# Score matmuls of a windowed attention, cut into 32 queries by the 96 keys that they see

## The chip, the cores and the metric

The kernel runs on one core of one Trainium2 chip. The metric is the device time of one execution in microseconds (us), as the median of several runs. The core has five engines that matter here: TensorE (PE in the profile, its weight loads PEld), VectorE (DVE), ScalarE (ACT), GpSimd (POOL) and SyncE (SP, which issues the DMA transfers).

## What is computed

```python
# q, k, v: (8 batches, 8 heads, 576 positions, 64), float32
scores = matmul(q, k^T) / sqrt(64)
rel = pos[:, None] - pos[None, :]
scores = where((rel >= 0) & (rel < 64), scores, -1e9)
attn = exp(scores - max(scores))
attn = attn / (sum(attn) + 1e-9)
x = matmul(attn, v), heads side by side           # (4608, 512)
h = maximum(x @ w_in, 0.0)                        # w_in (512, 2048)
out = (h * h) @ w_out                             # w_out (2048, 512)
```

A query sees itself and the 63 keys before it. So a block of 64 queries sees keys of its own block and of the block before, 128 in all; the first 32 queries of the block see only the first 96 of these, the last 32 only the last 96.

## The kernel before

The 4608 tokens are taken in 12 tiles of 384. Attention runs in sections: a section is four items, an item being one block of 64 queries of one batch for four heads (`d` picks the group of four, `j` and `hd` the head in it). A tile has three sections, so there are 36. Everything is one function, `section(op, i)`, with one letter per step:

- S, the scores (L227 to 238): for each item, for `j` and for `hd`, one 32-bit matmul of 64 queries by 128 keys (64 keys where the block is the first of its sequence). The head's 64 channels lie in partitions 0 to 63 or 64 to 127, and the output goes to partitions 0 to 63 or 64 to 127 of one of two PSUM banks: `half = hd ^ j`. So four neighbouring matmuls use the four 64x64 quarters of the 128x128 array.
- o and s (L246, L255, L256): ScalarE copies the scores of the own block out of PSUM, VectorE puts the scores of the block before over those that lie in the future. Each score that is kept comes from one of the two halves by the mask `late`.
- z, y, e, f, k, R, m: maximum (L258), exponential (L266), sum, reciprocal (L272), and on GpSimd the weighing by it (L275).
- X and x: TensorE transposes the weights (L279), VectorE masks them into `pt` (L283).
- V, the values (L301): 64 channels by 64 or 128 queries, again in 64x64 quarters.
- H and Q: the result leaves PSUM as operand of the feed-forward part (L316, L318).

The feed-forward part consists of wide products over the full array in a rounded 32-bit form with a high and a low part. Four tiles go the plain way: `mm1` (L407) and `mm2` (L449). The other eight go in pairs by seven products instead of eight: `product` (L940), `second` (L1038), and for the last pair `fast` (L1189).

What sets the order: up to about 190 us a list of tokens written out by hand (S, V, M for `mm1`, O for `mm2`, ...). After that a planner: `plan(engine, cost, do, reads, writes)` collects the steps; TensorE's steps keep the order in which they were planned, and each step of another engine gets a due time, which is the sum of TensorE's costs up to the step that needs it less its own cost. The earliest due goes first among those that are ready. `burst(i, j)` (L832) plans the scores of section i and right behind them the values of an earlier section j; `cross(i)` (L817) plans the transposes some products later.

```python
def scores(i):
    ...
    plan("pe", 0.85, by(section, "S", i), [("qk", d, j) for d in range(2) for j in range(2)], ["s_ps"])
...
def burst(i, j):
    scores(i)
    values(j)
    weigh(i)
    settle(j)
```

Of the kernel before, what the change touches and what calls it, by code (L numbers as in the profile page):

```python
# [14 lines left out]

P = 128
QB = 64
TB = 6
TT = QB * TB
SW = 4  # L20
# [9 lines left out]
def window_attention_relu2_ffn(ctx: ExitStack, tc: tile.TileContext, q, k, v, w_in, w_out, out):  # L30
    nc = tc.nc
    pe, dve, act, pool, sp = nc.tensor, nc.vector, nc.scalar, nc.gpsimd, nc.sync
    B, H, S, D = q.shape
    NT, DM = out.shape
    DF = w_in.shape[1] // 2
    NPAIR = H // 2
    NB = S // QB
    NF = DF // P
# [14 lines left out]
    banks = psum.tile([P, 8, DM], F32, name="banks")  # L53
    raw_t = att.tile([P, 2, 2, S], F32, name="raw")
    vt_t = att.tile([P, (NB + 1) // 2, 2, H // 2, D], F32, name="vt")
    qk_t = att.tile([P, 2, 2, 2, S], F32, name="qk")
    sel_t = att.tile([P, 2, SW, 2, QB], F32, name="sel")
    pt_t = att.tile([P, 2 * SW, P], F32, name="pt")
# [21 lines left out]

    late = const.tile([P, 1, QB], F32, name="late")
    masks = const.tile([P, 2, 2, QB], F32, name="masks")
    neg = const.tile([P, 1], F32, name="neg")
    nc.vector.memset(neg, NEG)
    for m, first_value, other, sign in ((late, 0.0, 1.0, 1), (masks[:, 1], 1.0, 0.0, -1), (masks[:, 0], 0.0, 1.0, -1)):
        nc.gpsimd.memset(m, first_value)
        for hd in range(2):
            rows = m[hd * QB:(hd + 1) * QB]
            nc.gpsimd.affine_select(out=rows, in_=rows, pattern=[[0, m.shape[1]], [-sign, QB]], base=0,
                                    channel_multiplier=sign, compare_op=ALU.is_ge, fill=other)  # L90
# [133 lines left out]
    def section(op, i, eng=None):  # L224
# [3 lines left out]
        if op == "S":  # L228
            ps = ps_s[i] = banks[:, 0:2]
            for w, (b, qb, d) in enumerate(items):  # L230
                c0 = 0 if qb else QB
                k0 = max(qb - 1, 0) * QB
                for j in range(2):
                    qk = (first[b][:, d] if b in first and qb < FIRST // QB else turned[b, d])[:, j]
                    for hd in range(2):
                        r = slice(hd * D, (hd + 1) * D)
                        half = hd ^ j
                        pe.matmul(ps[half * QB:(half + 1) * QB, j, w * P + c0:(w + 1) * P],  # L238
                                  lhsT=qk[r, 0, qb * QB:(qb + 1) * QB], rhs=qk[r, 1, k0:k0 + P - c0], start=True, stop=True)
            nms[i] = nm_t[:, 0, i % 3]  # L240
            sums[i] = nm_t[:, 1, i % 3]
        elif op in "os":
# [18 lines left out]
        elif op in "ef":  # L261
            for w in range(SW // 2):
                w += "ef".index(op) * SW // 2
                for hd in range(2):
                    n = slice(2 * w + hd, 2 * w + hd + 1)
# [7 lines left out]
        elif op == "m":  # L273
            p = sels[i].rearrange("p w h c -> p (w h) c")
# [11 lines left out]
        elif op == "V":  # L286

            ps = ps_x[i] = banks[:, 2:4]
# [6 lines left out]
            for m, (b, kb, d, n0, n) in enumerate(todo):  # L295
                q0 = n0 // 2 * QB
                for j in range(2):
                    for hd in range(2):
                        r = slice(j * QB, (j + 1) * QB)
                        half = hd ^ j  # L300
                        pe.matmul(ps[hd * D:(hd + 1) * D, j, q0:q0 + n * QB],  # L301
                                  lhsT=vts[b, kb // 2][r, kb % 2, 2 * d + hd, :],
                                  rhs=pts[i][r, n0:n0 + n, half * QB:(half + 1) * QB],
                                  start=m == 0, stop=m == len(todo) - 1, skip_group_check=True)
            pts.pop(i)
        else:
            hi, lo = get_x(i // SPT)
            ps = ps_x[i].rearrange("p m (w q) -> p m w q", q=QB)
            for d, nd, w0, r0, n in regions:
                cols = slice(r0 * QB, (r0 + n) * QB)  # L310
                h, l = hi[:, :, d:d + nd, cols], (hi if lo is None else lo)[:, :, d:d + nd, cols]
                vals = ps[:, :, w0:w0 + nd * n].rearrange("p m (d r) q -> p m d (r q)", d=nd)
                if nd == 1:
                    h, l, vals = h[:, :, 0], l[:, :, 0], vals[:, :, 0]
# [8 lines left out]
    def plan_tile(t):  # L323
        blocks = [divmod(t * TB + r, NB) for r in range(TB)]
        if t < 2:
            cuts = [[(d, r + n) for d in range(2) for n in range(2)] for r in range(0, TB, 2)]
        elif blocks[0][0] == blocks[-1][0]:
            order = [(d, r) for d in range(2) for r in range(TB)]
            cuts = [order[n:n + SW] for n in range(0, 2 * TB, SW)]
        else:  # L330
            cuts = [[(0, 0), (0, 1), (0, 2), (1, 0)], [(1, 1), (1, 2), (0, 3), (0, 4)], [(0, 5), (1, 3), (1, 4), (1, 5)]]
        for cut in cuts:
            at = [n for n, (d, r) in enumerate(cut) if blocks[r][1] == 0]
            if at and t > 1:
                cut = cut[at[0]:] + cut[:at[0]]
            regions = []
            for n, (d, r) in enumerate(cut):
                if n and cut[n - 1] == (d, r - 1):
                    regions[-1][4] += 1
                else:  # L340
                    regions.append([d, 1, n, r, 1])
            if len(regions) == 2 and regions[0][3:] == regions[1][3:]:
                regions = [[0, 2, 0, *regions[0][3:]]]
            yield [(*blocks[r], d) for d, r in cut], regions

    secs = [x for t in range(NTILE) for x in plan_tile(t)]
    SPT = 2 * TB // SW
    xt = {}
# [201 lines left out]
    with tc.manual_schedule(engines={E.PE, E.DVE, E.Activation, E.Pool, E.SP}):  # L550
        for token in order.split():
            op, eng = token[0], token[-1] if token[-1] in "dap" else None
            n = int(token[1:].rstrip("dap"))
# [8 lines left out]
            elif op == "D":  # L562
                turn(1 + n // NPAIR, n % NPAIR)
            elif op in "TU":
                ps_f[op, n] = turn_first("TU".index(op), *divmod(n, 2))
            elif op in "tu":
                copy_first("tu".index(op), *divmod(n, 2), ps_f[op.upper(), n], copier(eng))
            elif op == "K":
                idle(n)
            elif op == "P":  # L570
                fetch_w(0, n)
            elif op in "JjY":
                weight("abc"["JjY".index(op)], 0, half=n)
            elif op in "abcdhl":
                weight(op, n, eng)
            elif op == "M":
                hs[n] = mm1(*steps[n], lambda kk, part, f=steps[n][1]: wparts[f][:, 0, part, kk * P:(kk + 1) * P])
            elif op in "rpgG":
                evac(op, n, eng)
            elif op == "B":  # L580
                keep(n)
            elif op in "ACEF":
                mix(op, n)
            elif op in "OiI":
                mm2(*steps[n], *(gs[n] if op == "i" else gs.pop(n)), lambda part, f=steps[n][1]: wparts[f][:, 1, part],
                    {"O": range(NTB), "i": range(2), "I": range(2, NTB)}[op])
            elif op in "ZW":
                for tb in range(NTB):
                    put(op, steps[n][0], tb)
            else:  # L590
                section(op, n, eng)
# [134 lines left out]
    plan = Plan()  # L726

    def by(op, *args):
        return lambda: op(*args)
# [45 lines left out]
    def scores(i):  # L775
        if not SPT * 3 < i < SPT * NTILE:
            return
        plan("pe", 0.85, by(section, "S", i), [("qk", d, j) for d in range(2) for j in range(2)], ["s_ps"])

    def values(i):  # L780
        if SPT * 3 <= i < SPT * NTILE:
            plan("pe", 0.95, by(section, "V", i), ["pt"] + [("vt", t, n, m) for t in range(5) for n in range(2) for m in range(2)],
                 ["v_ps0", "v_ps1"])
# [48 lines left out]
# [5 lines that stand above are left out]
# [420 lines left out]
    for j in range(FULL):  # L1257
        for r in range(2 * SPT):
            i = SPT * NPLAIN + 2 * SPT * (j + 1) + r
            m = 16 * j + (2 * r if r else -4)  # L1260
            m, n = (0, (1, 4)) if m == 2 else (m, m + 1)
# [77 lines left out]
```

## Time and profile before

| | |
|---|---|
| time of the runs, us | 841.89, 841.23, 840.0 (median 841.23) |
| span of the profiled execution, us | 841.0 |
| TensorE matmul busy, us (share) | 826.7 (98%) |
| TensorE weight loads busy | 764.2 (91%) |
| VectorE busy | 620.5 (74%) |
| ScalarE busy | 435.2 (52%) |
| GpSimd busy | 242.7 (29%) |

The profile is of one execution; its own time is known by its span, from the first to the last instruction, which lies 0.2 us under the median. A 32-bit matmul (type f32 on both sides, not the rounded form) stands as two records in the profile, each with a weight load of its own. The first word pair of a PE row, as in `64*64 64x128`, is the part of the array that is used and then the output. "issue" is time in which an engine waited for nothing that the profile shows. Since matmuls are pipelined, starts tell more of the pace than durations.

### The profile page before, as it was taken

What the parts mean: (1) busy time and instruction counts of PE and PEld (TensorE: products, weight loads), DVE (VectorE), ACT (ScalarE), POOL (GpSimd) and SP (SyncE); (2) the same over time, 40 slices, a digit from 0 to 9 for tenths busy, and PEclk for the clock granted to TensorE, in tenths of its full rate; (3) what the DMA queues carried; (4) which work ended last, traced back from release to release, by engine and by line L of the source; (5) the groups of instructions that cost most, each with busy time, mean ns of one, the idle gap of its engine ahead of it and who ended that gap; (6) DMA issues with size and microseconds to landing.
All of it is one profiled execution on the core that took longest, in us unless ns stands there. A gap on an engine that the chain in (4) does not pass through costs nothing.

```text
span 841.0 us, 18284 instructions
## 1 busy us (share of the span) xinstructions
PE 826.7 (98%) x6928; PEld 764.2 (91%) x6928; DVE 620.5 (74%) x908; ACT 435.2 (52%) x1181; POOL 242.7 (29%) x313
## 2 busy tenths in 40 slices
PE   8799999999999999999999999999999999999998
PEld 6689899889999999999999999999999999999997
DVE  5899998467666867867777866788766759566876
ACT  6796774655546554544452455444355424455441
POOL 1220003024547520221251334252233452202121
PEclk9999999999999999999999999999999999999999
DMA  9999964737588894999896897999895866789842
GB/s 211 223 321 301 288 272 80 146 101 183 148 196 258 219 186 101 308 258 215 184 315 211 219 229 169 252 292 223 275 309 140 262 202 192 244 269 310 243 167 76
DMA packets 292264, 184.99 MB, mean 220 GB/s; under 512 B 191184, under 2 KB 257488, under 8 KB 290128
## 3 DMA queue, kind: packets, MB, share of 16 engines
q1 hardware_dynamic: 292176, 183.81, 78.6%
q8 instruction: 55, 0.90, 0.5%
q14 instruction: 33, 0.27, 0.1%
HBM read 142.87 MB, written 40.89 MB: 219 GB/s over the span
## 4 chain that ended last, share of the span: by engine, by line
PE 90%; DVE 3%; SPq 3%; ACT 2%; issue 1%; DMA 1%; POOL 0%; ACTq 0%; POOLq 0%
PE banks L940 26%; PE banks L1038 24%; PE banks L449 13%; PE banks L407 13%; PE banks L1189 5%; PE banks L238 4%; PE banks L301 3%; PE banks L279 2%; SPq L160 1%; ACT a L121 1%; DVE a L126 1%; SPq L188 1%; DMA w<-in_k_dram 1%; ACT sel L266 1%; SPq L107 1%
## 5 line engine op out<-in xcount | busy, mean ns | idle before, releaser
L1038 PE MATMUL banks<-w 128*128 128x512 f32 x888 | 199.8, 381 | 0.0
L1038 PEld LDWEIGHTS banks<-w 128*128 128x128 f32 x888 | 165.9, 189 | 21.6
L407 PE MATMUL banks<-x,w 128*128 128x384 f32 x768 | 137.9, 329 | 0.4 <-ACT r L416 0.4
L449 PE MATMUL banks<-w,g 128*128 128x512 f32 x576 | 136.1, 382 | 0.0
L407 PEld LDWEIGHTS banks<-x,w 128*128 128x128 f32 x768 | 125.9, 189 | 5.7 <-ACT r L416 2.3
L940 PE MATMUL banks<-x,w 128*128 128x384 f32 x768 | 130.3, 326 | 0.0
L940 PEld LDWEIGHTS banks<-x,w 128*128 128x128 f32 x768 | 125.6, 189 | 0.0
L449 PEld LDWEIGHTS banks<-w,g 128*128 128x128 f32 x576 | 106.4, 189 | 13.3 <-issue 0.3
L266 ACT ACTIVATE sel<-sel,nm 128x64 f32<-128x64 f32 x272 | 90.8, 336 | 22.3 <-DVE nm L260 21.9
L940 PE MATMUL banks<-w 128*128 128x384 f32 x576 | 100.7, 329 | 0.0
L970 POOL TENSOR_TENSOR g<-g 128x384 f32<-128x384 f32 x48 | 46.5, 973 | 180.5 <-ACT g L981 172.6
L940 PEld LDWEIGHTS banks<-w 128*128 128x128 f32 x576 | 93.4, 189 | 1.6
L1045 DVE TENSOR_TENSOR w<-w,banks 128x512 f32<-128x512 f32 (+1 forms) x61 | 41.1, 677 | 41.3 <-PE banks L1038 41.2
L416 ACT ACTIVATE r<-banks 128x384 f32<-128x384 f32 x64 | 31.2, 487 | 65.3 <-PE banks L407 59.9
L275 POOL TENSOR_TENSOR sel<-sel,nm 128x512 f32<-128x512 f32 x33 | 37.3, 1131 | 81.9 <-ACT g L981 31.9
L539 POOL TENSOR_TENSOR a<-w 128x256 f32<-128x256 f32 x28 | 24.4, 887 | 104.9 <-DVE w L135 75.0
L426 DVE TENSOR_TENSOR g<-r,g 128x384 fp32r<-128x384 f32 x64 | 38.2, 600 | 21.3 <-ACT g L424 14.4
L1022 ACT CAST w<-w 128x512 fp32r<-128x512 f32 x37 | 23.0, 621 | 56.3 <-PE banks L1038 56.3
L266 ACT ACTIVATION_READ_ACCUMULATOR sel<-sel,nm 128x1 f32 x272 | 51.1, 188 | 0.0
L283 DVE TENSOR_TENSOR pt<-banks,masks 128x1024 f32<-128x1024 f32 x33 | 40.2, 1219 | 9.1 <-PE banks L279 9.1
L958 DVE TENSOR_TENSOR w<-banks,r 128x384 f32<-128x384 f32 x64 | 38.3, 598 | 11.7 <-PE banks L940 11.2
L421 DVE TENSOR_TENSOR r<-r 128x384 f32<-128x384 f32 x38 | 24.7, 650 | 26.3 <-ACT r L416 26.2
(167 smaller groups left out, 1273.4 us busy)
## 6 DMA issues: line engine op xcount, KB each, us to landing
w<-mixed SPq DMA_DIRECT2D x128, 256.0 KB, 5.6
w<-kept SPq DMA_DIRECT2D x114, 256.0 KB, 6.1
w<-kept SPq DMA_DIRECT2D x52, 512.0 KB, 7.3
kept<-w SPq DMA_DIRECT2D x16, 1024.0 KB, 8.7
vt<-in_v_dram SPq DMA_DIRECT2D x144, 64.0 KB, 3.7
w<-in_moe_w_in_dram SPq DMA_DIRECT2D x16, 512.0 KB, 7.7
w<-in_moe_w_out_dram SPq DMA_DIRECT2D x16, 512.0 KB, 7.8
raw<-in_q_dram SPq DMA_DIRECT2D x112, 72.0 KB, 2.9
```

The source lines that it names most:

```text
L266: act.activation(sels[i][:, w, hd], sels[i][:, w, hd], AF.Exp, bias=nms[i][:, n], scale=SCALE, accum_out=sums[i][:, n])
L275: (dve if eng == "d" else pool).tensor_tensor(p, p, rs[i][:, :, None].broadcast_to([P, SW * 2, QB]), ALU.mult)
L283: dve.tensor_tensor(pts[i].rearrange("p (w n) q -> p w n q", n=2), ps_t[i][:, :, None, :].broadcast_to([P, SW, 2, P]), masks.rearrange("p ...
L407: pe.matmul(h_ps, lhsT=weights(kk, part), rhs=in_turn(x[xx][:, kk // 2, kk % 2]), start=n == 0, stop=n == 3 * NK - 1)
L426: (pool if eng == "p" else dve).tensor_tensor(gs[n][1], rg.pop(n), gs[n][0].bitcast(F32), ALU.subtract)
L449: pe.matmul(acc(t, tb), lhsT=gg[:, tb * P:(tb + 1) * P], rhs=in_turn(weights(part)), start=f == 0 and n == 0, stop=f == NF - 1 and n == 2)
L940: pe.matmul(ps[:, :TT], lhsT=w[:, part, kk * P:(kk + 1) * P], rhs=in_turn(x[:, xx, kk]), start=n < 4 and m == 0, stop=m == 5, skip_group_c ...
L958: plan("dve", 0.6, lambda: dve.tensor_tensor(to(), ps, other(), ALU.add), [kps, ko], keys, 0, after)
L970: plan("pool", 0.95, lambda: pool.tensor_tensor(x(), x(), x(), ALU.mult), [], keys)
L1038: pe.matmul(ps[:, :DM // parted], lhsT=gg[:, m // 2, m % 2], rhs=in_turn(wo_slot(w[m])[:, part, cols]), start=m == 0 and n == 0, stop=m == ...
L1045: plan("dve", 0.72 / parted, lambda ps=ps, to=to: dve.tensor_tensor(by_half(to()), by_half(to()), ordered(ps[:, :DM // parted]), ALU.add), ...
L1189: pe.matmul(ps[:, x * 2 * P:(x + 1) * 2 * P], lhsT=gg[:, st, x * P:(x + 1) * P], rhs=in_turn(w[:, st, part]), start=c == 0, stop=c == 5, s ...
```

## The change

`S` makes two matmuls out of each one: `u` picks 32 of the 64 queries, and of the 128 keys those 96 that they can see. The output goes to 32 partitions, so eight neighbouring matmuls use eight pieces of the array of 64 rows by 32 columns (two halves of rows, four strips of columns). In a first block the first 32 queries get 32 keys, the others 64. The two quarters of the scores that are no longer written are set to zero once at the start, by two memsets on VectorE. The planner's cost of a score section falls from 0.85 to 0.7.

```diff
--- before.py
+++ after.py
@@ -15,6 +15,7 @@
 
 P = 128
 QB = 64
+QS = QB // 2
 TB = 6
 TT = QB * TB
 SW = 4
@@ -82,6 +83,8 @@
     masks = const.tile([P, 2, 2, QB], F32, name="masks")
     neg = const.tile([P, 1], F32, name="neg")
     nc.vector.memset(neg, NEG)
+    nc.vector.memset(banks[:, 0:2].rearrange("p h (w n u c) -> p h w n u c", w=SW, n=2, u=2)[:, :, :, 1, 1], 0.0)
+    nc.vector.memset(banks[:, 0:2].rearrange("p h (w n u c) -> p h w n u c", w=SW, n=2, u=2)[:, :, :, 0, 0], 0.0)
     for m, first_value, other, sign in ((late, 0.0, 1.0, 1), (masks[:, 1], 1.0, 0.0, -1), (masks[:, 0], 0.0, 1.0, -1)):
         nc.gpsimd.memset(m, first_value)
         for hd in range(2):
@@ -235,8 +238,11 @@
                     for hd in range(2):
                         r = slice(hd * D, (hd + 1) * D)
                         half = hd ^ j
-                        pe.matmul(ps[half * QB:(half + 1) * QB, j, w * P + c0:(w + 1) * P],
-                                  lhsT=qk[r, 0, qb * QB:(qb + 1) * QB], rhs=qk[r, 1, k0:k0 + P - c0], start=True, stop=True)
+                        for u in range(2):
+                            first_c, last_c = max(c0, u * QS), P - (1 - u) * QS
+                            at, s0 = half * QB + u * QS, qb * QB + u * QS
+                            pe.matmul(ps[at:at + QS, j, w * P + first_c:w * P + last_c], lhsT=qk[r, 0, s0:s0 + QS],
+                                      rhs=qk[r, 1, k0 + first_c - c0:k0 + last_c - c0], start=True, stop=True)
             nms[i] = nm_t[:, 0, i % 3]
             sums[i] = nm_t[:, 1, i % 3]
         elif op in "os":
@@ -775,7 +781,7 @@
     def scores(i):
         if not SPT * 3 < i < SPT * NTILE:
             return
-        plan("pe", 0.85, by(section, "S", i), [("qk", d, j) for d in range(2) for j in range(2)], ["s_ps"])
+        plan("pe", 0.7, by(section, "S", i), [("qk", d, j) for d in range(2) for j in range(2)], ["s_ps"])
 
     def values(i):
         if SPT * 3 <= i < SPT * NTILE:
```

What it moves. TensorE, the planned part, one section of full blocks with the values behind it: L940 and L1038 (L946 and L1044 after) are the wide products, L279 (L285) the transposes, L238 (L244) the scores, L301 (L307) the values. Before:

```order
L940 MATMUL banks<-x_2043,w 128x384 x12
L279 MATMUL banks<-ident,sel 128x128 x4
L940 MATMUL banks<-x_3612,w 128x384 x12
L238 MATMUL banks<-qk 64x128 x16
L301 MATMUL banks<-pt,vt 64x128 x8
L301 MATMUL banks<-pt,vt 64x64 x12
L940 MATMUL banks<-w 128x384 x18
L940 MATMUL banks<-x_2043,w 128x384 x12
L940 MATMUL banks<-x_3612,w 128x384 x12
```

and after the change:

```order
L946 MATMUL banks<-x_2221,w 128x384 x12
L285 MATMUL banks<-ident,sel 128x128 x4
L946 MATMUL banks<-x_3950,w 128x384 x12
L244 MATMUL banks<-qk 32x96 x32
L307 MATMUL banks<-pt,vt 64x128 x8
L307 MATMUL banks<-pt,vt 64x64 x12
L946 MATMUL banks<-w 128x384 x18
L946 MATMUL banks<-x_2221,w 128x384 x12
L946 MATMUL banks<-x_3950,w 128x384 x12
```

The sequence is the same; 16 score matmuls of 64x128 have become 32 of 32x96, and the values stand right behind them as before. A section with a first block has eight matmuls of 32x32 and 32x64 in turn, then 24 of 32x96. In the whole order 26 of the 36 score sections have the values directly behind, 25 of them after 62 us, 15 of these without a first block and ten with one; of the five others after 62 us two have one.

GpSimd, early in the planned part with paired tiles: L275 (L281) is the weighing of a section's attention, L970 (L976) the squares of the hidden layer, L892 (L898) sums of operands. Before:

```order
L275 TENSOR_TENSOR sel<-sel,nm 128x512
L970 TENSOR_TENSOR g<-g 128x384 x2
L275 TENSOR_TENSOR sel<-sel,nm 128x512
L970 TENSOR_TENSOR g<-g 128x384
L275 TENSOR_TENSOR sel<-sel,nm 128x512
L970 TENSOR_TENSOR g<-g 128x384 x2
L892 TENSOR_TENSOR w<-a 128x768
```

and after the change:

```order
L281 TENSOR_TENSOR sel<-sel,nm 128x512
L976 TENSOR_TENSOR g<-g 128x384 x2
L281 TENSOR_TENSOR sel<-sel,nm 128x512
L976 TENSOR_TENSOR g<-g 128x384 x2
L281 TENSOR_TENSOR sel<-sel,nm 128x512
L976 TENSOR_TENSOR g<-g 128x384
L898 TENSOR_TENSOR w<-a 128x768
```

The third weighing shown stands one square later than before. Such moves are all there is on the other engines, when each instruction is compared with its like: 47 of GpSimd's 319 stand elsewhere, by six places at most; on VectorE 91 of 911 (the L170 transposes of q and k among them) by eight at most; on ScalarE 74 of 896 by ten at most; on SyncE 41 of 816 (loads of weights, of `mixed`, of q and k) by fifteen at most.

## Rows read from the trace of the kernel before

**Rows 1.** The page, parts 1, 2 and 4: engine, busy us (share of the span), records
```profile
PE 826.7 (98%) x6928; PEld 764.2 (91%) x6928; DVE 620.5 (74%) x908; ACT 435.2 (52%) x1181; POOL 242.7 (29%) x313
...
PEclk9999999999999999999999999999999999999999
...
PE 90%; DVE 3%; SPq 3%; ACT 2%; issue 1%; DMA 1%; POOL 0%; ACTq 0%; POOLq 0%
```

**Rows 2.** Table of stretches: us, busy us (records) by engine, clock, DMA share, GB/s
```profile
0.00:62.00 62.00, 51.42 (x653) 44.46 (x657) 49.38 (x71) 48.08 (x146) 13.08 (x29) 0.97 0.96 250
62.00:143.00 81.00, 80.58 (x467) 73.56 (x460) 75.76 (x82) 53.12 (x82) 7.68 (x12) 1.00 0.75 242
...
190.00:600.00 410.00, 410.00 (x3562) 379.56 (x3555) 300.44 (x475) 200.84 (x614) 143.78 (x181) 1.00 0.86 223
```

**Rows 3.** Waits of TensorE from 55 us on: us in total, times, longest us
```profile
engine line waited for: us in total, times, longest us
PE banks L279 <- POOL sel L275: 1.3, 1, 1.3
PE banks L407 <- ACT r L416: 0.4, 1, 0.4
```

**Rows 4.** Timeline, 43.9 to 47.2 us: start us, us, engine line op out<-in xcount
```profile
44.22 1.10 PE L238 MATMUL banks<-w 64*64 64x128 f32 x32
...
44.85 0.52 ACT L419 ACTIVATE r<-r 128x384 f32<-128x384 f32 x1
...
45.39 0.59 ACT L246 COPY sel<-banks 128x512 f32<-128x512 f32 x1
```

**Rows 5.** The chain of waits, 62 us on: start us, us, what
```profile
349.62 7.02 PE banks L940 x42
```

**Rows 6.** Timelines of one score section, 347.4 to 349.9 us (PE matmuls, PEld weight loads)
```profile
347.48 0.33 PE L940 MATMUL banks<-x,w 128*128 128x384 f32 x1
347.73 0.34 PE L238 MATMUL banks<-qk 64*64 64x128 f32 x4
...
347.73 0.15 PEld L238 LDWEIGHTS banks<-qk 64*64 64x64 f32 x4 [0.23 <-issue]
...
348.66 0.96 PE L301 MATMUL banks<-pt,vt 64*64 64x128 f32 x40
...
349.09 0.53 PE L301 MATMUL banks<-pt,vt 64*64 64x64 f32 x24
349.55 0.59 PE L940 MATMUL banks<-w 128*128 128x384 f32 x2
...
348.44 0.15 PEld L238 LDWEIGHTS banks<-qk 64*64 64x64 f32 x4
348.55 0.93 PEld L301 LDWEIGHTS banks<-pt,vt 64*64 64x64 f32 x40
349.55 0.30 PEld L940 LDWEIGHTS banks<-w 128*128 128x128 f32 x2
```

**Rows 7.** Groups by shape from 62 us on: busy us, mean ns | idle before
```profile
L238 PE MATMUL banks<-qk 64*64 64x128 f32 x864 | 30.1, 274 | 0.0
...
L238 PE MATMUL banks<-qk 64*64 64x64 f32 x96 | 4.5, 243 | 0.0
```

**Rows 8.** Timeline of a values section of 64-wide matmuls, 54.3 to 55.8 us
```profile
54.58 0.79 PEld L301 LDWEIGHTS banks<-pt,vt 64*64 64x64 f32 x48 [0.23 <-DVE pt L283]
54.59 0.93 PE L301 MATMUL banks<-pt,vt 64*64 64x64 f32 x48
...
55.44 0.51 PEld L449 LDWEIGHTS banks<-w,g 128*128 128x128 f32 x3
```

**Rows 9.** Timeline of PE, 301.9 to 303.3 us: a section with a first block, then values
```profile
302.30 1.00 PE L238 MATMUL banks<-qk 64*64 64x64 f32 x32
303.12 0.40 PE L301 MATMUL banks<-pt,vt 64*64 64x128 f32 x8
```

**Rows 10.** Timeline of weight loads, 35.8 to 36.2 us
```profile
35.68 0.27 PEld L301 LDWEIGHTS banks<-pt,vt 64*64 64x64 f32 x12
36.02 0.26 PEld L199 LDWEIGHTS banks<-ident,w 64*128 64x128 f32 x3
```

**Rows 11.** Timeline of VectorE from the start
```profile
0.86 0.06 DVE L84 MEMSET neg<- 128x1 f32 x1 [0.86 <-PEq L1322]
6.18 0.69 DVE L205 COPY qk<-banks 128x512 f32<-128x512 f32 x1 [5.27 <-PE banks L199]
```

## The prediction

> **What bounds the kernel now.** Read the page's shares first [rows 1]: TensorE is busy for 98% of the span, its clock stands at full speed, and it holds 90% of the chain that ended last. Then the table of stretches [rows 2]: up to 62 us VectorE and ScalarE carry 49.4 and 48.1 us of work and TensorE idles for over 10; from 190 to 600 us TensorE never idles. Then its waits [rows 3]: from 55 us on only 1.7 us end on another engine. So a nanosecond taken off TensorE's stream after 62 us comes off the end, and one taken off earlier does not: the section at 44.2 us, for one, hands its scores to a ScalarE that is busy until 45.37 and copies at 45.39 [rows 4].
>
> A busy TensorE still hides pauses, because the modelled ends overlap them. They show in the starts [rows 6]. The last wide product before a score section starts at 347.48; such products follow each other every 7.02/42 = 0.167 us [rows 5], so its columns are through at 347.64, yet the first score weights load at 347.73. This is a pause of 0.09 with no engine waited for ("issue").
>
> **What a section costs now.** After 62 us there are 864 + 96 = 960 score records [rows 7]. A 32-bit matmul leaves two, so a section of 16 matmuls leaves 32, and 30 sections lie there; the 96 short ones are twelve first blocks of a sequence, with 64 keys and eight records each. Records start in fours: four stand within the 0.03 us after 347.73 [rows 6]. The pace of four follows from the values matmuls of the same shape: sixteen records from 348.66 to 349.09, so 0.43/4 by stamps rounded to 0.01; I take 0.109. Two passes over 128 keys at 2.4 GHz are 0.107, so all four 64x64 tiles of the array work at once, with 0.002 lost per turn. Eight turns make 0.875; from the first load at 347.73 to the first values record at 348.66 are 0.93, so the first load costs 0.05. With 64 keys, twelve turns and a first load take 0.85 [rows 8], six turns 0.46 [rows 6], each with the same pause at its end: 0.34 / 6 = 0.057 per turn. A section with a first block takes 0.82 before its values start [rows 9].
>
> **The change, part by part.** *Columns.* 32 matmuls leave 64 records over 96 keys, eight side by side: two passes are 0.080, with the same loss 0.0825, eight turns 0.66 instead of 0.875. In a first block the slower tile still sees 64 keys, two turns of 0.057; with six of 0.0825 that is 0.61. *The first load* brings 32 queries instead of 64: 0.03 instead of 0.05 (half, an estimate).
>
> *The tile shape.* Scores and values now share one shape, 64*64, and the values weights follow at 348.55, 0.11 after the last score loads, at the running pace: no pause [rows 6]. After the change scores run as 64*32 and values as 64*64. What a change between two divided shapes costs shows once: values end and a transpose in shape 64*128 begins [rows 10]. The loads there end at 35.95 and the next starts at 36.02, 0.07 later, exactly the step from values to wide products (349.48 to 349.55, [rows 6]). So I charge the full pause, 0.09, plus the values' first load that was hidden, 0.05: 0.14 per section whose values follow directly. The bounds are 0, if these two shapes need no pause, and 0.17, since by starts the values-to-wide pause is 349.55 - (349.09 + 6 x 0.057) = 0.12. The Trainium skill, TensorEngine Tiling (Array Packing), section Tiling Modes, Key Properties, says that a change of tiling mode, not only of tile, drains TensorE; the traces' 0.07 agrees, and this rule speaks against the change.
>
> *The sum after 62 us.* PE's order has 25 sections with values right behind and 5 without. Fifteen of the 25 are full: 0.93 becomes 0.03 + 0.66 + 0.14 = 0.83, 0.10 saved each, 1.5 together. Ten hold a first block: 0.82 becomes 0.78, 0.4 together. Of the five, three save 0.93 - 0.69 = 0.24 and two 0.82 - 0.64 = 0.18: 1.1. In all 3.0 us.
>
> *Two memsets.* VectorE is idle for 5.27 us before its first copy at 6.18 and the first score needs that copy; 256 columns each, half the width of that copy (0.69), so 0.7 for both [rows 11]. Nothing on the path; without the cover 0.7.
>
> *The planned order.* The smaller cost shifts due times: some SyncE loads, VectorE transposes and GpSimd weighings move, by fifteen places at most; PE's own order stays. GpSimd's weighing is what TensorE once waited for, 1.3 us [rows 3]; I charge nothing, since every other such wait is covered, and 1.3 per wait if one opens. No load is waited for by TensorE after 55 us [rows 3], which covers SyncE's swaps.
>
> The profiled span is 841.0 us, the three runs' median 841.23, 0.2 above it. 841.2 - 3.0 = **838.2**; with the pause between 0.07 and 0.12 and small shifts 837 to 839.6.
>
> **Rivals.**
> 1. *No pause between 64*32 and 64*64.* Then 25 x 0.14 more comes off: 838.2 - 3.5 = 834.7. For it: both keep 64 rows. Against: 64*128 keeps them too and pauses [rows 10].
> 2. *A wait takes the gain.* Two weighings that come late at 1.3 us each: 838.2 + 2.6 = 840.8, no change. For it: GpSimd's rows are the ones that move. Against: only one such wait now.
> 3. *Slower: the records can't be issued so fast.* 64 pairs of load and matmul in 0.66 us are one per 10.3 ns. The densest stretch now, 48 pairs in twelve turns of 0.057, is one per 14.3 ns [rows 8], and there columns set the pace; four start within 0.03, under 10 ns each, but in bursts. At that pace a section takes 0.915: the 15 lose 0.155, the ten 0.265, the three 0.015, the two 0.125, 5.3 in all: 841.2 + 5.3 = 846.5. The gain is gone at 11.5 ns. The Trainium skill, TensorE: Matmul & The Clock Gate, section "Wait — 56ns, not 53.3ns?", says that starts never come closer than about 25 ns however few the columns; by that a section would take 1.6 and the sum 867 (an estimate from the page). The trace disagrees: 48 records in 0.7 us.
> 4. *Only four tiles stream at once,* since four column strips now draw on the same 64 rows where two did. Then a section takes 1.32: against before 0.57 is lost in each of 25 and 0.42 in each of 5, 16.3, 857.5. For it: no row shows more than four. Against: four tiles now lose only 0.002 a turn.
>
> **How the numbers follow.** My forecast 0.52, rival one 0.12, two 0.12, three 0.14, four 0.10. A measurement tells some 0.2%, 1.7 us, from no change. Faster: 0.46 of the forecast's 0.52 and rival one, 0.58. Same: the rest of the forecast, rival two and 0.02 of three (a pace near 11.5), 0.20. Slower: 0.22. The range takes in the forecast and rivals one to three, 0.90, from 834.3 to 846.8; without rival three it would hold under 0.8.
>
> **What would show it.** Right: score records in turns of eight, 0.08 apart; 0.69 from first load to last turn; then a gap of about 0.09 before the first values load, and TensorE's waits unchanged. Wrong: values loads that follow without a gap (one), new waits on GpSimd (two), records spaced evenly over 0.1 per eight (three), turns of four (four).

## The result: 1.3% slower

| | before | after |
|---|---|---|
| median of the runs | 840.62 us (4 runs, 839.99 to 841.89) | 850.95 us (4 runs, 849.85 to 852.92) |
| ratio, 95% interval | | 1.0126 [1.0109, 1.0143] |
| profiled execution: its own time, its span | span 841.0 us | 849.85 us, span 848.1 us |

The forecast was 838.2 us and its range ended at 846.8; the change lost 10.3 us instead of gaining 3.

The page after, parts 1, 2 and 4, against [rows 1]. The columns are engine, busy us (share of the span) and records, then the granted clock in 40 slices, then the chain's shares.

```profile
PE 829.3 (98%) x8080; PEld 762.7 (90%) x8080; DVE 623.2 (73%) x910; ACT 435.7 (51%) x1181; POOL 241.7 (28%) x313
...
PEclk9999999999999998999999999999999999999999
...
PE 88%; DMA 3%; SPq 3%; DVE 3%; ACT 2%; issue 1%; POOL 0%; DVEq 0%; ACTq 0%; POOLq 0%
```

There are 1152 more TensorE records, 32 more in each of 36 sections. The shares hardly move, but one slice of the clock does, the sixteenth, near 320 us. TensorE's waits from 55 us on, against [rows 3] (us in total, times, longest):

```profile
engine line waited for: us in total, times, longest us
PE banks L413 <- ACT r L422: 6.5, 2, 6.1
PE banks L285 <- POOL sel L281: 1.2, 1, 1.2
```

GpSimd's wait is the old one (lines have moved by 3 to 6). ScalarE's is new: one wait of 6.1 us. The table of stretches finds it, against [rows 2], where 190 to 600 us had no idle time:

```profile
core 0: us, PE busy (x) PEld busy (x) DVE busy (x) ACT busy (x) POOL busy (x), PEclk, DMA share, GB/s
...
190.00:600.00 410.00, 403.88 (x4070) 370.87 (x4069) 294.64 (x462) 198.03 (x607) 142.28 (x181) 0.99 0.84 217
300.00:340.00 40.00, 33.88 (x394) 30.28 (x393) 21.28 (x31) 16.95 (x43) 4.41 (x7) 0.91 0.58 129
```

All 6.1 us lie between 300 and 340 us, and the clock is down to 0.91 there. Three timelines of after (start us, us, engine, line, operation, count, and in brackets the idle time and what ended it) tell what happened. TensorE:

```profile
308.69 2.11 PE L413 MATMUL banks<-x,w 128*128 128x384 f32 x12
...
324.01 3.63 PE L413 MATMUL banks<-x,w 128*128 128x384 f32 x12 [6.12 <-ACT r L422]
```

ScalarE, whose relu of the first product (L422) TensorE waits for:

```profile
322.21 0.62 ACT L551 CAST a<-a 128x512 fp32r<-128x512 f32 x1 [9.11 <-DMA mixed<-a]
322.74 0.83 ACT L909 CAST w<-w 128x768 fp32r<-128x768 f32 x1
323.47 0.48 ACT L422 ACTIVATE r<-banks 128x384 f32<-128x384 f32 x1
```

SyncE's queue:

```profile
308.30 0.46 SPq L153 DMA_DIRECT2D raw<-in_q_dram  x1
...
311.66 6.67 SPq L163 DMA_DIRECT2D vt<-in_v_dram  x8
318.44 0.55 SPq L555 DMA_DIRECT2D mixed<-a  x1
```

Read from the last fence upwards. The store of mixed operand 12 (`mix("F", 12)`, L555) is issued at 318.44, behind eight value loads that take 6.67 us. ScalarE's cast of operand 14 (L551) writes the same staging buffer, so it waits until the store has been read out, 9.11 us. Behind the cast in ScalarE's order stands the relu, and TensorE cannot go on without it. In the kernel before, the store stood ahead of the query, key and value loads, and the same cast began with no wait:

```profile
302.13 2.73 SPq L549 DMA_DIRECT2D mixed<-a  x1
304.96 0.69 SPq L740 DMA_DIRECT2D w<-kept  x1
```

```profile
312.22 0.60 ACT L545 CAST a<-a 128x512 fp32r<-128x512 f32 x1
```

The clock adds to it. Stretches of after, TensorE alone (busy us, granted clock, DMA share, GB/s):

```profile
318.00:320.00 2.00, 0.00 (x0) 1.00 0.56 136
320.00:322.00 2.00, 0.00 (x0) 0.52 1.08 261
322.00:324.00 2.00, 0.00 (x0) 0.50 0.94 150
324.00:326.00 2.00, 1.99 (x6) 0.50 0.64 102
326.00:328.00 2.00, 2.00 (x10) 0.77 0.00 0
```

TensorE falls idle at 317.9; from 320 us on the granted clock is 0.5 of 2.4 GHz, the 1.2 GHz level, and it is back only some 3 us after work resumes. The twelve products at 324.01 take 3.63 us where twelve took 2.11: 1.5 us on top of 6.1.

The score section itself, against [rows 6]:

```profile
353.23 0.65 PE L946 MATMUL banks<-x,w 128*128 128x384 f32 x3
...
353.81 0.78 PEld L244 LDWEIGHTS banks<-qk 64*32 64x32 f32 x64 [0.23 <-issue]
353.81 1.00 PE L244 MATMUL banks<-qk 64*32 64x96 f32 x64
...
354.73 1.01 PE L307 MATMUL banks<-pt,vt 64*64 64x128 f32 x40
...
355.68 0.59 PE L946 MATMUL banks<-w 128*128 128x384 f32 x2
```

From the first score record to the first values record are 0.92 us, as before (0.93 by starts in [rows 6]), though each record has a quarter fewer columns. So the columns did not come back either. The starts of that section's records, in us after the first, show why:

```
records  1 to  8   0.000 0.007 0.014 0.020 0.027 0.034 0.040 0.047
records  9, 17, 25 0.107 0.189 0.272    (each with seven more behind it, 0.007 apart)
record  33         0.354
first passes then  0.385 0.402 0.419 0.435 0.452 0.469 0.485 ...  (second passes between them)
last eight         0.657 0.670 0.671 0.689 0.705 0.721 0.739 0.754
```

Half of the records go in turns of eight, 0.0825 us apart, as forecast. From the 34th on new matmuls begin 0.0167 us apart, each with its second pass some time later, and the last passes too trail out 0.017 apart. The last record starts at 0.754; in regular turns it would start at 0.649. The spacing alone would not cost that: eight records in 0.067 us are quicker than a turn of 0.0825. The row of new matmuls begins late; the experiments show what it is behind.

### The profile page after: what moved, and what is told of

Same layout as the page of the kernel before. It is cut to its first block, busy times and chain, and to the rows that moved or that the text cites. A ratio compares the mean times of both kernels' runs of the same rounds, so it can differ in the third digit from the quotient of the medians.

```text
span 848.1 us, 20589 instructions
## 1 busy us (share of the span) xinstructions
PE 829.3 (98%) x8080; PEld 762.7 (90%) x8080; DVE 623.2 (73%) x910; ACT 435.7 (51%) x1181; POOL 241.7 (28%) x313
## 4 chain that ended last, share of the span: by engine, by line
PE 88%; DMA 3%; SPq 3%; DVE 3%; ACT 2%; issue 1%; POOL 0%; DVEq 0%; ACTq 0%; POOLq 0%
PE banks L946 26%; PE banks L1044 24%; PE banks L455 12%; PE banks L413 12%; PE banks L1195 5%; PE banks L307 4%; PE banks L244 3%; PE banks L285 2%; SPq L163 1%; DMA w<-in_moe_w_out_dram 1%; DMA vt<-in_v_dram 1%; SPq L191 1%; DVE a L131 1%; DVE a L129 1%; SPq L110 1%
## 5 line engine op out<-in xcount | busy, mean ns | idle before, releaser
L1044 PE MATMUL banks<-w 128*128 128x512 f32 x888 | 199.8, 381 | 0.0
L1044 PEld LDWEIGHTS banks<-w 128*128 128x128 f32 x888 | 165.9, 189 | 21.6
L946 PE MATMUL banks<-x,w 128*128 128x384 f32 x768 | 130.3, 326 | 0.0
L946 PEld LDWEIGHTS banks<-x,w 128*128 128x128 f32 x768 | 125.6, 189 | 0.0
L976 POOL TENSOR_TENSOR g<-g 128x384 f32<-128x384 f32 x48 | 44.4, 925 | 226.6 <-ACT g L987 215.4
L946 PE MATMUL banks<-w 128*128 128x384 f32 x576 | 100.7, 329 | 0.0
L946 PEld LDWEIGHTS banks<-w 128*128 128x128 f32 x576 | 93.4, 189 | 1.6
L422 ACT ACTIVATE r<-banks 128x384 f32<-128x384 f32 x64 | 31.1, 485 | 65.4 <-PE banks L413 60.0
L281 POOL TENSOR_TENSOR sel<-sel,nm 128x512 f32<-128x512 f32 x33 | 37.5, 1138 | 55.7 <-DVE nm L278 33.2
L1028 ACT CAST w<-g 128x512 fp32r<-128x512 f32 x36 | 22.2, 621 | 42.2 <-PE banks L1044 42.2
```

The source lines that it names most:

```text
L946: pe.matmul(ps[:, :TT], lhsT=w[:, part, kk * P:(kk + 1) * P], rhs=in_turn(x[:, xx, kk]), start=n < 4 and m == 0, stop=m == 5, skip_group_c ...
L976: plan("pool", 0.95, lambda: pool.tensor_tensor(x(), x(), x(), ALU.mult), [], keys)
L1028: plan("act", 0.62, lambda: act.copy(homes()[0], src()), g_keys, [kh], 0, freed("hi") if new else [])
L1044: pe.matmul(ps[:, :DM // parted], lhsT=gg[:, m // 2, m % 2], rhs=in_turn(wo_slot(w[m])[:, part, cols]), start=m == 0 and n == 0, stop=m == ...
```

## The experiments

The two effects can be tried apart, since the planner's cost and the matmuls are two edits. For the TensorE part I use one measure beside the runs' medians: the starts of the score sections from the first one after 100 us, compared with before. Up to that mark (144.5 us in before) the order is written by hand, and up to 62 us engines other than TensorE bind, so times there vary more. All entries are us later (+) or earlier than the kernel before, counted from that mark:

| kernel | at 302 us of before | at 332 us | at 514 us | at the end | median, us |
|---|---|---|---|---|---|
| after | -0.02 | +7.87 | +8.50 | +9.06 | 850.95 |
| split_cost85 | -0.04 | +0.05 | +0.70 | +1.24 | 843.83 |
| whole_cost70 | 0.00 | +7.72 | +7.72 | +8.05 | 848.78 |
| whole_store_late | 0.00 | +6.56 | +6.56 | +6.58 | 845.6 |
| split_store_early | -0.04 | +0.05 | +0.69 | +1.99 | 843.2 |
| split_alternate | -0.06 | +0.01 | +0.63 | +1.16 | 842.37 |
| split_128keys | +1.71 | +1.91 | +3.84 | +5.53 | 846.92 |
| split_64keys | -1.47 | -1.47 | -1.84 | -2.24 | 839.08 |
| whole_96keys | -2.36 | -2.53 | -4.23 | -5.77 | 834.38 |

**The order and the split apart.** split_cost85 is the changed kernel with the planner's old cost, so that every engine but TensorE keeps the order of before:

```
-        plan("pe", 0.7, by(section, "S", i), ...
+        plan("pe", 0.85, by(section, "S", i), ...
```

> The split matmuls with the planner's old cost of 0.85, so that every engine but TensorE has the order of before. Order theory (the loss comes from the order that the cost of 0.7 brings): the 6.1 us wait of TensorE on ScalarE near 320 us and the clock's drop are gone; by the starts of the two traces the split alone loses 0.05 us in each of 15 sections and 0.09 in each of 10, and gains 0.1 in each of 5, so 1.3 us net after 62 us, less whatever the early part gains (0 to 1.9): 840 to 842.5 beside 840.6. Split theory (the loss lies in TensorE's own pace): 849 to 852 as after the change.

843.83 us (12 runs), ratio 1.0035 [1.0023, 1.0048]. Its waits from 55 us on:

```profile
PE banks L285 <- POOL sel L281: 1.2, 1, 1.2
PE banks L413 <- ACT r L422: 0.4, 1, 0.4
```

The new wait is gone, and with it 7 us. What is left is still slower than before. whole_cost70 is the converse: the kernel before, with 0.7 in place of 0.85 and nothing else.

> The whole matmuls of before with the planner's cost of 0.7, so that the other engines have the order of the changed kernel. Order theory: TensorE waits 5 to 7 us for ScalarE once near 320 us, its clock falls to half after that, 848 to 853. Split theory: no such wait, 840 to 841.5.

848.78 us (6 runs), ratio 1.0092 [1.0073, 1.0111], with the new wait:

```profile
PE banks L407 <- ACT r L416: 5.7, 2, 5.4
```

So the planner's cost alone, without a single changed matmul, makes most of the loss: by the table +7.72 at one place.

**Which instruction.** split_store_back is the changed kernel with the store of operand 12 put back where SyncE had it before, behind the store of operand 15:

```
+        store = dos[tags.index(("mix", "F", 12))]
+        dos.remove(store)
+        dos.insert([...].index(("mix", "F", 15)) + 1, store)
```

> The changed kernel with one step put back: the store of the twelfth mixed operand stands ahead of the 7 loads of q, k and weights and the 8 loads of v again, as before; nothing else of the order differs from the changed kernel. If this store alone makes the wait: as split_cost85 within 1 us, and no wait of TensorE over 2 us after 55 us. If other moves of the order share in it: 845 or more, or the wait stands elsewhere.

853.97 us (5 runs), ratio 1.0152 [1.0132, 1.0173]: worse. The old wait has gone and a larger one stands elsewhere:

```profile
PE banks L285 <- ACT a L322: 9.3, 1, 9.3
```

VectorE's timeline of this kernel gives the reason:

```profile
310.91 0.69 DVE L553 TENSOR_TENSOR a<-a 128x512 fp32r<-128x512 f32 x1 [12.23 <-DMA mixed<-a]
```

In the changed order VectorE's subtraction that ends operand 12 (`mix("E", 12)`) comes later than that place. The store therefore went out ahead of it, with the low-order half that stood in the buffer before, and the subtraction had to wait for the store. The edit was faulty as a test: a store cannot be moved back without what it stores. Two better ones followed. whole_store_late makes the delay alone, in the kernel before (whole matmuls, cost 0.85): SyncE's store of operand 12 goes behind the eight value loads.

```
+        store = dos[tags.index(("mix", "F", 12))]
...
+        loads = [n for n in range(at, len(dos)) if tags[n][:1] == ("load_v",)]
+        dos.insert(loads[7] + 1, store)
+        del dos[at]
```

> The kernel before with that one store put behind the 8 loads of v, nothing else moved. If the store alone makes the wait: TensorE waits 4 to 7 us for ScalarE between 315 and 330 us, the clock falls to half for some us, 845 to 852. If it takes more than the store: within 1 us of 840.6.

845.6 us (7 runs), ratio 1.0057 [1.0037, 1.0076], and the wait is there again, shorter:

```profile
PE banks L407 <- ACT r L416: 3.8, 2, 3.5
```

ScalarE's cast is held by the same store, and the relu stands behind it:

```profile
316.48 0.62 ACT L545 CAST a<-a 128x512 fp32r<-128x512 f32 x1 [5.89 <-DMA mixed<-a]
317.00 0.48 ACT L416 ACTIVATE r<-banks 128x384 f32<-128x384 f32 x1
```

Its entry in the table, +6.56, is of an execution of 847.5 us, the second longest of its seven; by the medians of that batch the store costs 5.2 us (845.6 against 840.4).

split_store_early takes the delay alone away, in the changed kernel:

```
+        store = dos.pop(tags.index(("mix", "F", 12)))
+        low_at = [k for k, t in enumerate(tags) if t[:3] == ("mix", "E", 12)][-1]
+        dos.insert(low_at + 1, store)
```

> The changed kernel as it is (cost 0.7), with one instruction moved: the store of mixed operand 12 stands right behind the subtraction that ends it (E of 12), so ahead of the four query and key loads and the eight value loads that stand before it in the changed kernel; every other instruction of the other engines keeps its place. Theory (the 6.1 us wait comes from this store standing behind those loads): the store lands before 314 us, ScalarE's cast of operand 14 no longer waits, TensorE's waits after 55 us fall from about 7.7 us to under 2.5 us, the clock no longer falls near 320 us, and the time is that of the split with the order before, 843.8 us, give or take 1 us. Rival (the other moves of the order cost as much by themselves, as the earlier attempt to move the store back seemed to say): a wait of over 3 us is left within 300 to 330 us and the time is above 847 us.

843.2 us (12 runs), ratio 1.0027 [1.0016, 1.0037]. The waits are those of split_cost85, and SyncE and ScalarE show the store ahead of the value loads again and the cast held for 0.33 us:

```profile
310.57 0.53 SPq L555 DMA_DIRECT2D mixed<-a  x1
...
315.69 5.35 SPq L163 DMA_DIRECT2D vt<-in_v_dram  x8
```

```profile
314.52 0.62 ACT L551 CAST a<-a 128x512 fp32r<-128x512 f32 x1 [0.33 <-DMA mixed<-a]
```

One DMA issue, moved by twelve places on SyncE, is the difference between 850.95 and 843.2 us. The other moves of the order cost nothing that shows.

**Why the split alone doesn't pay.** Four kernels with the order of before vary the columns, the records and the tiles. whole_96keys takes away the columns without splitting anything:

```
+                        n = (P - c0) * 3 // 4
-                        pe.matmul(ps[half * QB:(half + 1) * QB, j, w * P + c0:(w + 1) * P], ...
+                        pe.matmul(ps[half * QB:(half + 1) * QB, j, w * P + P - n:(w + 1) * P], ...
```

> The kernel before with each score matmul of 64 queries cut to 96 of its 128 keys (first blocks to 48 of 64), nothing split; the scores of the 32 other keys are left out (zero in the banks). This takes away the columns that the change takes away, without more records and without another tile shape. Theory (a turn of four at 96 columns takes 0.0825 us, 20.6 ns per pair, well over the 13.6 ns at which pairs can be issued, so TensorE's sections after 62 us give the columns back one for one): first to last start 0.63 us instead of 0.835 us, 30 x 0.205 = 6.2 us less, 834.1 us. Rival (the time that TensorE saves turns into waits for other engines, or the shorter sections are held by issuing as well): 837 us or more.

834.38 us (5 runs), ratio 0.9926 [0.9914, 0.9938], within 0.3 us of the theory. A section now, to be set against 0.93:

```profile
341.96 0.89 PE L240 MATMUL banks<-qk 64*64 64x96 f32 x32
342.67 0.60 PE L303 MATMUL banks<-pt,vt 64*64 64x128 f32 x13
```

That is 0.71. Its 32 records go in turns of four, 0.0825 us apart, from the second turn to the end. So the premise was sound: columns taken from TensorE after 62 us come off the end. split_128keys does the reverse, the split without fewer columns:

```
-                            first_c, last_c = max(c0, u * QS), P - (1 - u) * QS
+                            first_c, last_c = c0, P
```

> Two matmuls of 32 queries as in the change, each by all 128 keys (first blocks 64), with the cost at 0.85 so that the other engines' order is that of before: as many columns for a pair of matmuls as before go through eight tiles instead of four, 64 record pairs a section. Theory (a section is held by its columns, 0.0825 us per turn of eight at 96 keys, for the first records and by about 13.6 ns per record pair later): a turn of eight at 128 keys takes 0.110 us or 13.7 ns per pair, so the first to the last start takes 0.86 to 0.88 us instead of 0.754 us, and the 30 sections after 62 us add 30 x 0.12 = 3.6 us to the split at 843.8 us: 847.4 us. Rival (the pace of issuing alone holds the section): first to last start stays near 0.75 us and the time near 843.8 us.

846.92 us (6 runs), ratio 1.0070 [1.0057, 1.0084], beside 847.4 expected:

```profile
348.37 1.16 PE L244 MATMUL banks<-qk 64*32 64x128 f32 x64
349.45 0.45 PE L307 MATMUL banks<-pt,vt 64*64 64x128 f32 x8
```

The turns of eight begin 0.109 us apart, so eight 64*32 tiles do stream at once. From the 38th record on the starts within a turn spread out to 0.0167 us here too, and the last one, at 0.887 us, is 0.05 late. From the first score to the first values record are 1.08 us instead of 0.93. split_64keys goes the other way:

```
+                            first_c, last_c = max(c0, u * QB), P - (1 - u) * QB if c0 == 0 else P - (1 - u) * QS
```

> Two matmuls of 32 queries, each by 64 of the 128 keys (first blocks 32), cost 0.85; the scores of the other keys are left out (those cells of the banks stay at zero). The records stay 64 a section, the columns of each fall by a third. Theory (the first half of a section goes by its columns, the second half by the pace at which load and matmul pairs are issued, 13.6 ns): 32 records at 0.055 us per turn of eight (0.22 us) and 32 at 13.6 ns (0.435 us), so first to last start about 0.64 us instead of 0.754 us, and 30 sections x 0.11 us take 3.3 us off the split at 843.5 us: 840.2 us. Rival (columns hold the whole section): 64 records at 0.055 us per turn, 0.44 us, 9.4 us off: 834.1 us.

839.08 us (12 runs), ratio 0.9980 [0.9967, 0.9993]. By the table it is 3.5 us quicker than split_cost85 (-2.24 against +1.24); the theory said 3.3 and the rival 9.4.

```profile
344.60 0.86 PE L243 MATMUL banks<-qk 64*32 64x64 f32 x64
345.39 0.45 PE L306 MATMUL banks<-pt,vt 64*64 64x128 f32 x8
```

First to last start is 0.643 us (0.64 expected). Within it the first 32 records take 0.268 us and the other 32 0.375, where 96 columns took 0.354 and 0.40: with fewer columns the first half shrinks and the second hardly does. In that half the new matmuls again start 0.0167 us apart. The pace I had written down, 13.6 ns per record, is no pace of issuing: 0.40/32 is 12.5 ns, and two records every 0.0167 us would be 8.3.

What holds the second half shows when the three kernels are set side by side, in us from the first record of a section. A matmul is two records, so the first matmul's second one is the ninth to start; its end is the profile's modelled one. The row of new matmuls 0.0167 apart begins with the weight load of the eighteenth matmul:

```
keys   ninth record starts, ends   load of the eighteenth matmul
 64    0.080  0.296                0.328
 96    0.107  0.349                0.381
128    0.134  0.403                0.434
```

The load comes 0.03 us behind the end of the first matmul, whatever the columns, and so it does in all 18 full sections after 62 us of these three kernels, of split_cost85 and of split_alternate (30 to 33 ns). At 96 and 128 keys the 26th matmul's load stands as far behind the end of the ninth matmul (0.514 and 0.546 at 96 keys). So a new matmul comes only after the one seventeen before it has ended; sixteen lie between. At 96 keys and in regular turns the eighteenth's load would stand at 0.281 instead of 0.381, and the section's last record is 0.105 late. A section of 16 matmuls never gets there by itself. split_alternate asks whether the pace comes from two loads after another on the same rows:

```
-                    for hd in range(2):
+                    for u in range(2):
...
-                        for u in range(2):
+                        for hd in range(2):
```

> The split as in the change with cost 0.85, with the loops over the two heads and the two halves of the queries exchanged, so that consecutive matmuls lie on different rows of the array (0 to 63, 64 to 127) instead of two after another on the same rows. Theory (the pace of the second half is that of issuing, whatever tile comes next): first to last start stays at 0.75 us, time at 843.5 us. Rival (two loads after another on the same rows hold each other up): the second half goes at the column pace too, first to last start 0.66 us, 30 x 0.09 = 2.8 us less: 840.7 us.

842.37 us (11 runs), ratio 1.0018 [1.0006, 1.0030]; first to last start 0.755 us, the same 0.0167 between starts. Which rows come next does not matter.

**Where the rest of the 3 us lies.** By the table split_cost85 loses 1.24 us from the mark on, but its median is 3.5 above before. Two kernels divide it:

```
split_early, whole matmuls in the sections after 62 us:
+                        if not (i < 6):
+                            pe.matmul(ps[half * QB:(half + 1) * QB, j, w * P + c0:(w + 1) * P], ...
split_late, whole matmuls in the first six sections:
+                        if not (i >= 6):
```

> The split in the first six sections only (those before 62 us), whole matmuls in the 30 later ones, cost 0.85, so the order of the other engines is that of before. The split with that order took 843.8 us, 3.4 us over before, and of this only about 1.3 us is found in its sections after 62 us. Theory (the other 2 us arise before 62 us): 842.3 us, 2 us over before. Rival (the early sections have slack, and all 3.4 us arise later): 840.4 us, as before.

> The counterpart: whole matmuls in the first six sections, the split in the 30 sections after 62 us, cost 0.85. Theory (only the sections' own lengthening counts after 62 us: 15 x 0.053 + 10 x 0.093 - 3 x 0.107 - 2 x 0.068 = 1.3 us): 841.7 us. Rival (all of the 3.4 us arise after 62 us): 843.8 us.

split_early 841.35 us, ratio 1.0015 [1.0000, 1.0030]; split_late 842.35 us, ratio 1.0024 [1.0010, 1.0039]. Neither rival holds: the loss lies in both parts, some 1 us early and 2 us late, and the intervals are as wide as the shares. For the early share the runs' mean clocks give a reason. In the six kernels that split the first six sections and have no wait near 320 us, 46 of 65 executions have a mean granted clock of 0.998 or less; in split_late, split_no_values, whole_96keys and the runs of before beside them it is 22 of 104. split_early's seven executions with such a clock have a median of 842.1 us, its five others 840.3, as before. The stretches of split_early and then split_late (TensorE):

```profile
33.00:36.00 3.00, 2.61 (x120) 0.77 0.97 262
36.00:40.00 4.00, 3.68 (x31) 0.74 0.81 213
```

```profile
33.00:36.00 3.00, 2.35 (x57) 1.00 0.97 264
36.00:40.00 4.00, 3.06 (x24) 1.00 0.75 195
```

Some 3.4 us at the 1.2 GHz level, in the part in which TensorE idles for 10 us anyhow [rows 2]. So the split there goes with a clock that falls more often. Less score work alone does not: whole_96keys has it too, with 0 of 5, and split_128keys, split without fewer columns, has 2 of 6. Why the clock falls in one execution and not in another I did not find. For the late share, the longer sections make some 1.2 us, as in split_cost85. split_late's profile ends 2.24 later than before, 1.0 more than split_cost85, and between 525 and 595 us it has small waits that split_cost85 lacks:

```profile
PE banks L950 <- DMA w<-mixed: 0.5, 2, 0.3
```

The last kernel tried for a gain: whole matmuls, with the split only in the five sections that no values follow.

```
+                        if not (i in (6, 7, 8, 9, 13)):
```

> The kernel before, with the split in those five sections alone that no value section follows (the seventh to tenth and the fourteenth), cost 0.85. In the changed kernel these five became shorter, three by 0.107 us and two by 0.068 us. Theory: 0.46 us less after 62 us, 839.8 us against 840.3 us, which the runs can hardly tell from no change; the stretch from the first section after 100 us to the end, 696.5 us before, reads 696.0 us. Rival (mixed kinds cost something at the change from one to the other): 696.5 us or more.

840.86 us (12 runs), ratio 1.0012 [0.9996, 1.0028]: not told from before. By the table's measure it stands at -0.43 us from 302 to 514 us, just what was forecast; then a wait on a load of the mixed weights takes it back (+1.72 at the end):

```profile
PE banks L950 <- DMA w<-mixed: 1.3, 1, 1.3
```

No kernel that computes all the scores beat the kernel before.

## Why the prediction was wrong

**The planned order: wrong, and the larger part.** The step "I charge nothing" rested on the sentence that no load is waited for by TensorE after 55 us, "which covers SyncE's swaps". It looked at loads, and at who waits for them directly. The instruction that hurt was a store. TensorE waits for no store; ScalarE's cast waits for this one, because both use one staging buffer, and TensorE waits for what stands behind the cast. The list of moves ahead of the prediction names SyncE's as loads; by the traces two of the 41 are stores, and the one that moves by fifteen places is this store. The cover was there to be read: before, the store was issued 10 us ahead of the cast (302.13 and 312.22 above), and eight value loads alone take over 5 us of SyncE. Priced by the runs: +7.72 of the +9.06 in the table (whole_cost70, the order alone), confirmed by whole_store_late (the store alone, +6.56 there, 5.2 by the medians) and split_store_early (the store put right, 7.75 us back).

**Columns: wrong in the second half of each section.** "Eight turns 0.66" held for four turns. Then the eighteenth matmul waits for the end of the first, and the 26th for that of the ninth. Rival three, which I gave 0.14, was right that the records do not come fast enough, for half of them, but not by a fixed pace of issuing. The last record ends at about 0.754 + 0.08 = 0.83 us instead of 0.025 + 0.66 = 0.685, so each full section loses 0.15 against the forecast. By starts, from the last wide product ahead to the second one behind, a full section typically grew by 0.053 where 0.10 was to come off, one with a first block grew by 0.093 instead of shrinking by 0.04, and the five without values gained 0.107 (three) and 0.068 (two) where 0.24 and 0.18 were forecast. Summed: 15 x 0.053 + 10 x 0.093 - 3 x 0.107 - 2 x 0.068 = 1.27 us, and split_cost85's table entry is +1.24. No row of the kernel before could show this limit: its sections have 16 matmuls, and those of whole_96keys too, which go in regular turns to the end. "Four start within 0.03, but in bursts" said only that starts can lie close as long as matmuls are at hand.

The floor of 25 ns between starts that the prediction took from the Trainium skill (TensorE: Matmul & The Clock Gate, section "Wait — 56ns, not 53.3ns?") does not show here either: starts are 7 ns apart in a burst and 17 ns from the eighteenth matmul on. The same page of the Trainium skill (section "Architectural detail: the array is 16× 32×32, not 1× 128×128") gives TensorE a queue of 64 entries. The sixteen matmuls between one that ends and the one that is let in are 32 records with a load each, 64 in all, which fits it; no run here shows the queue itself.

**First load and tile shape: right.** The first turn takes 0.107 instead of 0.0825, so 0.025 for the first load (0.03 forecast). The first values record starts 0.173 us after the last score record; a record lasts 0.08, so the pause is 0.09 as charged, and the first values turn then takes 0.160 instead of 0.109, the 0.05 for the load that is no longer hidden. Rival one falls. The rule of the Trainium skill that the prediction set beside it (TensorEngine Tiling (Array Packing), section Tiling Modes, Key Properties) agrees.

**Rival four** falls: split_128keys runs eight tiles in 0.109 us.

**Rival two** named the right kind, a wait that takes the gain, and the wrong engine.

**Two memsets at nothing: not contradicted.** With both memsets split_late reaches the mark at 141.91 us, whole_cost70 without them at 141.70; times at this mark vary by more than that.

**The sum's base: 1.5 us off.** I set the profiled span, 841.0, beside the median as if both were run times. A run is its span and some 1.7 us more (849.85 and 848.1 above), so that profile was of one of the longer executions, with the clock at half near 31 us. It changed no sign.

## What to carry to other kernels

When a change alters a cost in a planner, compare the order it writes on every queue, stores included, and for each moved transfer ask who next writes the buffer that it reads: that engine's whole queue stands behind it. A cost of 0.7 instead of 0.85 looked like a correction of a model and was worth 8 us, so try the order and the arithmetic apart. And before small matmuls are split into more of them, look whether the records still come in regular turns at the end of a run, and not only at its start.

## What was not expected of the hardware

- Many short matmuls in a row run into a limit that few do not. The first 16 matmuls of a section start 7 ns apart in turns of eight; the eighteenth's weight load comes only 30 to 33 ns behind the end of the first matmul, at 64, 96 and 128 columns, on the same rows or on others, and the next ones follow 16.7 ns apart. Against regular turns the last record of a section is then late by 0.18 us at 64 columns, 0.10 at 96 and 0.05 at 128.
- TensorE was idle from 317.9, the clock was at 1.2 GHz from 320 us, and it stayed there for about 3 us of renewed work. A wait of 6.1 us so cost 7.6.
- In a part of the program where TensorE already idles, splitting its matmuls went with a lower clock in more executions: 46 of 65 against 22 of 104. Which part of the split does it isn't shown.
